# Other transfer times in a kernel's order model, and the ranks that go with them: delta rule and low-rank mixer on one core

## The chip, the core and the metric

The kernel runs on one NeuronCore of a Trainium2 chip. The metric is device microseconds (us) of one execution; a kernel's time is the median of its runs. An execution that the profiler recorded has a time of its own, and its span, from the first to the last instruction, is a little shorter than that.

## What is computed

Two blocks, one after the other, all in float32. The first is a delta-rule recurrence over 768 tokens for 4 batches with 8 heads of 48 numbers each. The second is a mixer: a low-rank product over the tokens, and then a two-layer network over the channels.

```python
k_n = k / (norm(k) + 1e-6)                     # q, k, v: (4, 8, 768, 48)
for t in range(768):
    y[:, :, t] = q_t @ state                   # state: (4, 8, 48, 48), zero at first
    state = state + beta_t * outer(k_n_t, v_t - k_n_t @ state)
x = y with the heads side by side              # (4, 768, 384)
u = x + (U @ V applied over the tokens of x)   # rank 32
out = u + relu(u @ w_ch1) @ w_ch2              # 384 -> 1536 -> 384
```

The weights of the mixer (U, V, w_ch1, w_ch2) come as 64-bit floats, and the kernel converts them to 32 bits itself.

## The kernel before

**Stages.** The recurrence is done in chunks of 64 tokens. A unit n is half of a batch: 6 chunks of all 8 heads; there are 8 units, two for each batch. For each unit the kernel loads k, q, v and a second copy of part of k that it calls z (`load`: 28 DMAs of 72 KB for a unit, 8 each for k, q and v, 4 for z), turns k and q with TensorE (`turn` in `grams`, L475, evicted at L485 to L490), forms the products within the chunks (`products`, L502, evicted at L512 to L533), inverts 32x32 triangles on VectorE (`blocks`: the transpose L584, the scaling L588, a loop of pairs L593 and L599, the transpose back L606), joins the pieces on TensorE (`joins`, L615 to L716), and multiplies the result into k and v (`prepare`, L808 and L819). Norms and beta come in through `norms` (L441 to L458; L458 scales v, and so waits for the loads of v) and `load_beta` (L410 to L425). The recurrence itself (`recur`) goes from chunk to chunk: L857 on TensorE, L870 on VectorE, L885 on TensorE, L895 on VectorE (L897 in chunk 0); `outputs` (L772, L786, L756) hangs on it. When all 12 chunks of a batch are there, `front` (L1180 to L1209) and `wide` (L1288, L1328) do the mixer in three blocks of 256 tokens for a batch; the last batch has another form for the first layer (`quick`, L1085).

**Weights.** `load_weights` brings the weights in as 14 slices: slice 0 is U, slice 1 is V (`v_sb`, 4 DMAs of 192 KB), slices 2 to 7 are w_ch1 and 8 to 13 are w_ch2 (2 DMAs of 384 KB each). `start(i)` issues slice i (L967), and can do so when slice i-1 has been issued and the buffer is free again. VectorE converts each in five steps (L989, L995, L1001, L1007, L1017), ScalarE does one between (L974). Sums of w_ch2 follow on VectorE (`sums`, L925).

**What sets the order.** Every engine executes its instructions in the order in which the program lists them, and that order is written by a planner that runs when the program is built. Each part above is a Python generator; it yields an operation with an engine and an estimated cost, or a list of events that it needs. `run()` keeps a clock for each engine, takes at each step the operation that can start first and, among those that can start within 0.18 us of the first, the one with the lowest rank. The rank is given to `begin(part, place)`, and the table `PLACES` replaces it for the parts that it names. So a table and the estimated costs make the order; what the chip does later has no say in it, and an instruction whose input is late holds all that is behind it on its engine.

A DMA's landing is estimated by `landing`: one server for all queues, 1.0 us after the issue at the earliest, a time for each packet, and 0.4 us behind it. An issue from SyncE (SP) or GpSimd (POOL) costs 0.65 us in the model. Where a load is at SP, the parts that are ready compete by rank: the loads of k, q, v, z of the first two units have the ranks 10 to 17 by default (`FIRST`), the slices of weights 22, the recurrence 1 for batch 0 and 59 for the others, `wide` 95.

Of the kernel before, what the change touches and what calls it, by code (L numbers as in the profile page):

```python
# [26 lines left out]
def kernel(  # L27
# [72 lines left out]
    def op(  # L100
        engine, cost, mode=None, take=None, give=(), lat=None, rush=None, words=0, port=None, flow=None
    ):
        return dict(
            flow=cost * 0.95 if flow is None else flow,
            e=engine, cost=cost, mode=mode, take=take, give=give, words=words + 0.4,
            port=engine == "pool" if port is None else port,
            rush=bool(give) if rush is None else rush, lat=LAT[engine] if lat is None else lat,
        )

    def need(*keys):  # L110
        return [key for key in keys if key[1] >= 0]

    def emitted(key, after=0.0):
        done[key] = state["now"] + after
        for i in awaited.pop(key, ()):
            missing[i].discard(key)
            if not missing[i]:
                woken.append(i)

    def landing(packets, each=0.0235):  # L120
        state["hw"] = max(state["hw"], state["now"] + 1.0) + packets * each / 16
        return state["hw"] + 0.4 - state["now"]

# [14 lines left out]
            waits[i] = s  # L138

    PLACES = """  # L140
    add_up b1 i1 45.09; blocks n3 111.0; blocks n4 92.42; blocks n6 79.19
    front b1 i2 64.0; front b2 i2 68.2; grams n1 i1 1.0; grams n3 i0 53.42
    grams n3 i1 -4.5; grams n4 i0 45.18; joins n0 h1 45.17; joins n1 h0 15.27
    joins n2 h0 -4.0; joins n2 h1 7.5; joins n5 h1 18.5; joins n6 h0 60.13
    joins n6 h1 68.5; joins n7 h1 62.0; last_sum b0 i2 80.69; load n0 nameq halves(0, 1) 75.0
    load n0 namez halves(0, 1) 3.5; load n1 namez halves(0, 1) 92.5; load n5 namek halves(0, 1) 49.53; load n5 namez halves(0, 1) 92.89
    load n6 namek halves(0, 1) 68.35; load_beta u0 51.5; load_beta u1 90.62; load_weights 88.45
    norms n1 113.0; norms n2 108.5; norms n3 19.33; norms n5 46.0
    outputs b0 c0 94.0; outputs b0 c3 15.7; outputs b0 c5 84.5; outputs b1 c6 56.12
    outputs b2 c0 87.54; outputs b2 c5 58.09; outputs b3 c0 -10.5; outputs b3 c1 51.03  # L150
    outputs b3 c4 81.5; outputs b3 c6 78.5; prepare n0 h0 99.5; prepare n0 h1 78.37
    prepare n1 h0 80.0; prepare n2 h0 -1.5; prepare n2 h1 6.5; prepare n3 h0 8.5
    prepare n5 h0 7.5; prepare n5 h1 44.42; prepare n6 h1 43.06; products n0 i0 j0 97.01
    products n0 i0 j1 82.0; products n0 i1 j1 110.0; products n1 i1 j1 53.69; products n2 i0 j1 73.87
    products n3 i0 j1 31.11; products n4 i0 j0 55.59; products n4 i0 j1 57.63; products n4 i1 j0 57.63
    products n5 i1 j1 3.5; products n6 i0 j1 100.7; products n6 i1 j0 73.37; products n6 i1 j1 47.56
    products n7 i1 j0 59.09; products n7 i1 j1 86.0; recur b0 31.68; recur b1 19.99
    recur b3 22.0; seed n6 -8.0; start i1 113.77; wide b0 i0 65.24
    wide b0 i2 73.0; wide b1 i2 115.5; wide b2 i1 76.0
    """  # L160
    PLACES = dict(x.strip().rsplit(" ", 1) for x in PLACES.replace("\n", ";").split(";") if x.strip())

# [115 lines left out]
    def half(i, size=L):  # L278
        return slice(L * i, L * i + size)

    def quarter(i, size=BK):
        return slice(BK * i, BK * i + size)
# [78 lines left out]
    def load(n, name, halves):  # L361
        kn, _, _, _, qn, vn, _, kz = units[n]
        t, src = dict(k=(kn, k), q=(qn, q), v=(vn, v), z=(kz, k))[name]
        b, hf = divmod(n, NU)
        yield need(("rec", n - 2), *[("x", b - 1, UC * hf + c) for c in range(UC)])
        if name == "v":
            yield need(("turned", n))
        if name == "k" and n == 0:
            e = "sp" if halves == (0,) else "act"
        else:  # L370
            e = "sp"
        for g in halves:
            if n >= NU and g:
                e = "pool"
            queue = dict(sp=nc.sync, act=nc.scalar, pool=nc.gpsimd)[e]
            for s in range(1, 4, 2) if name == "z" else range(4):
                to = dict(k=s, q=s, v=s % 2 * 2 + s // 2, z=s // 2)[name]
                yield op(e, 0.65, port=False)
                queue.dma_start(  # L379
                    out=t[half(1 - g if name == "z" else g), :, to, 0:D],  # L380
                    in_=src[b, 4 * g + s, hf * UC * L : (hf + 1) * UC * L, :].rearrange(
                        "(c t) d -> t c d", t=L
                    ),
                )
                after = landing(384)
                if name == "z" or s % 2:
                    emitted((name, n, g, s // 2), after)
        if len(halves) == 1 and halves[0]:
            yield op("act", 1.6)
            nc.scalar.sqrt(warm, warm)  # L390

    def load_beta(u):
# [3 lines left out]
        if u == 0:  # L396
            for g in range(2):
                yield op("pool", 0.6, port=False)
                nc.gpsimd.dma_start(out=beta_sb[:, g], in_=beta[:, 4 * g : 4 * g + 4])
            yield op("pool", 0.0, port=False, lat=landing(64, 0.1))  # L400
        else:
            yield need(("gram", 0))
# [150 lines left out]
    def halves(t, split):  # L553

        size = BK // split
        flat = t.rearrange("p a b -> p (a b)")[:, 0 : split * size * (BK + (split > 1))]
        return flat.rearrange("p (u x) -> p u x", u=split)[:, :, 0 : size * BK].rearrange(
            "p u (a b) -> p u a b", b=BK
        )[:, :, :, 0:size]
# [371 lines left out]
    def load_weights():  # L931
# [11 lines left out]
        def size(i):  # L943
            return NB * R if slices[i][2] == "c" else WIDE

        def start(i):
            _, src, kind = slices[i]
            n = size(i)
            before = max([x for x in range(i) if where[x] == where[i]], default=-1)
            yield need(("started", i - 1), ("freed", before), *[("joined", 0)] * (where[i] == 2))  # L950
            to = wides[where[i]][:, 0 : 2 * n]
            landed[i] = to.rearrange("p (n two) -> p n two", two=2)
            src = src.bitcast(I32)
            if kind == "c":
                pieces = [(to.rearrange("p (c r) -> p c r", c=NB), src.rearrange("(c p) r -> p c r", c=NB))]
            elif kind == "a":
                to = to.rearrange("p (t f x) -> p t f x", t=KT, f=2)
                pieces = [(to[:, :, f], src[:, :, f]) for f in range(2)]
            elif kind == "f":
                to = to.rearrange("p (a f d) -> p f a d", a=2, f=2)  # L960
                pieces = [(to[:, f], src[f]) for f in range(2)]
            else:
                pieces = [(to[quarter(j)], src) for j in range(128 // R)]
            e, queue = ("pool", nc.gpsimd) if i < 1 else ("sp", nc.sync)
            for to, of in pieces:
                yield op(e, 0.6, port=False)
                queue.dma_start(out=to, in_=of)  # L967
            emitted(("started", i))
            emitted(("wide", i), landing(256, 0.13) + 0.6)

        def raised(i, power):
            cost = 0.16 + size(i) * 0.001
# [9 lines left out]
        for i in range(len(slices)):  # L982
# [3 lines left out]
            wide = landed.pop(i)  # L986
# [349 lines left out]
    with tc.manual_schedule():  # L1336
        begin(load(0, "k", (0,)), 3)
        begin(load(0, "k", (1,)), 3)
        begin(load_beta(0), 4)
        begin(load_beta(1), 16)  # L1340
        for b in range(B):
            begin(recur(b), 1 if b == 0 else 59)
        for n in range(N):
            begin(norms(n), place_of(n))
            begin(grams(n, 0), place_of(n))
            begin(grams(n, 1), place_of(n) + 3)
            begin(blocks(n), place_of(n))
            for y, name in enumerate("kqvz"):
                if n or y:
                    begin(load(n, name, (0, 1)), FIRST.get((name, n), 20 + 4 * n + y))  # L1350
        begin(load_weights(), 40)
        begin(reserve(), 0)
        begin(weight_sums(), 97)
        begin(token_sums(), 3)
        begin(first_of_last(), 94)
        for b in range(B):
            for i in range(NG):
                begin(front(b, i), 2)
        for b in range(B):
            for i in range(NG):  # L1360
                begin(wide(b, i), 95)
        run()
# [30 lines left out]
```

## Time and profile before

| | us |
|---|---|
| median of 3 runs (lowest, highest) | 617.05 (615.25, 617.24) |
| profiled execution, its own time | 622.36 |
| its span | 620.6 |
| TensorE busy | 584.3 (94%) |
| VectorE busy | 418.3 (67%) |
| ScalarE busy | 235.6 (38%) |
| GpSimd busy | 81.5 (13%) |
| mean granted clock of TensorE | 0.929 |

A busy time is the sum of an engine's instructions in the span. The page also cuts the span into 40 slices of 15.5 us and gives the busy share of each in tenths; the granted clock of TensorE is given as a share of full speed. A wait names the instruction that waited, and the one whose end released it. The first products of the mixer (L1288) start at 125.83 us.

### The profile page before, as it was taken

How to read it: one execution, taken by the hardware profiler on the slowest of the kernel's cores; microseconds unless marked ns; L12 is line 12 of the kernel's file. 1: busy time of each engine (PE TensorE's matmuls, PEld its weight loads, DVE VectorE, ACT ScalarE, POOL GpSimd, SP SyncE). 2: the span in 40 equal slices, each digit the busy share in tenths (PEclk: the TensorE clock that was granted, in tenths of full speed). 3: DMA queues.
4: the chain of work that ended last, by engine and by line, in shares of the span. 5: the costliest groups of instructions: out<-in, count | busy, mean ns of one | idle time of the engine just before them, and what ended most of it. 6: DMA issues, size and time to landing. Idle time of an engine off the chain costs nothing.

```text
span 620.6 us, 23281 instructions
## 1 busy us (share of the span) xinstructions
PE 584.3 (94%) x10452; PEld 502.8 (81%) x10452; DVE 418.3 (67%) x1000; ACT 235.6 (38%) x462; POOL 81.5 (13%) x145
## 2 busy tenths in 40 slices
PE   5767968899999999999999999999999999999997
PEld 4666967689889889788988978988989878755997
DVE  6968979688988817899887359968972235132542
ACT  4735654651044174246327323353134131244000
POOL 3001006410000230151025032010010000000000
PEclk9766565799999999999999999999999999999999
DMA  6560549940000240370034043000000000000001
GB/s 125 107 160 5 170 154 201 207 107 2 27 5 3 61 65 4 69 131 4 3 74 91 3 96 57 11 29 3 3 28 2 27 2 2 25 2 0 6 36 36
DMA packets 72293, 33.26 MB, mean 54 GB/s; under 512 B 59649, under 2 KB 70657, under 8 KB 72193
## 3 DMA queue, kind: packets, MB, share of 16 engines
q1 hardware_dynamic: 66400, 24.98, 18.1%
q0 software_dynamic: 4192, 6.49, 4.9%
q8 instruction: 82, 1.34, 0.9%
q10 hardware_dynamic: 1600, 0.30, 0.3%
q14 instruction: 19, 0.15, 0.1%
HBM read 27.03 MB, written 4.72 MB: 51 GB/s over the span
## 4 chain that ended last, share of the span: by engine, by line
PE 84%; DVE 7%; issue 3%; ACT 2%; DMA 2%; SPq 2%; DVEq 0%; ACTq 0%
PE P L1328 27%; PE P L1288 23%; PE P L1085 7%; PE P L502 4%; PE P L475 3%; PE P L1198 3%; PE P L857 3%; DMA slot<-in_k_dram 2%; PE P L808 2%; PE P L819 2%; PE P L885 2%; PE P L772 2%; SPq L379 2%; PE P L1207 1%; PE P L786 1%
## 5 line engine op out<-in xcount | busy, mean ns | idle before, releaser
L1288 PE MATMUL P<-ut,w_sb 128*128 128x256 f32 x648 | 153.8, 386 | 0.0
L1288 PEld LDWEIGHTS P<-ut,w_sb 128*128 128x128 f32 x648 | 119.6, 191 | 19.0 <-issue 1.9
L1328 PE MATMUL P<-w_sb,hs 128*128 128x192 f32 x540 | 95.1, 330 | 0.0
L1328 PEld LDWEIGHTS P<-w_sb,hs 128*128 128x128 f32 x540 | 87.3, 190 | 1.6
L599 DVE TENSOR_TENSOR xt<-xt,prod 128x112 f32<-128x112 f32 (+21 forms) x200 | 64.5, 323 | 6.9
L1264 DVE TENSOR_TENSOR X<-X,P 128x192 f32<-128x192 f32 x84 | 29.6, 352 | 58.4 <-PE P L1328 57.3
L756 ACT COPY X<-P 64x192 f32<-64x192 f32 x96 | 30.1, 314 | 101.9 <-PE P L786 99.7
L593 DVE TENSOR_TENSOR prod<-gs,xt 128x112 f32<-128x112 f32 (+21 forms) x200 | 63.9, 320 | 4.5
L1231 ACT ACTIVATE hs<-P 128x512 f32<-128x512 f32 x54 | 32.2, 597 | 82.0 <-PE P L1288 78.6
L1328 PE MATMUL P<-w_sb,S 128*128 128x192 f32 x288 | 50.2, 329 | 0.0
L1328 PEld LDWEIGHTS P<-w_sb,S 128*128 128x128 f32 x288 | 46.7, 190 | 0.5
L475 PE MATMUL P<-ident,slot 128*128 128x128 f32 x192 | 31.5, 314 | 11.2 <-DMA slot<-in_k_dram 7.4
L870 DVE TENSOR_TENSOR z<-slot,P 128x192 f32<-128x192 f32 x44 | 15.5, 353 | 35.2 <-PE P L857 32.2
L728 ACT COPY slot<-zz 32x384 f32<-32x384 f32 x64 | 32.5, 509 | 14.9 <-DVE X L1264 8.6
L475 PEld LDWEIGHTS P<-ident,slot 128*128 128x128 f32 x192 | 25.9, 162 | 14.6 <-issue 8.1
L502 PEld LDWEIGHTS P<-slot 48*64 48x64 f32 x1536 | 28.8, 151 | 6.9 <-ACT slot L490 3.2
L502 PE MATMUL P<-slot 48*64 48x64 f32 x1536 | 32.4, 238 | 1.7 <-ACT slot L490 1.4
L1085 PE MATMUL P<-slot,w_sb 128*128 128x384 f32 x96 | 33.3, 486 | 0.0
L379 POOL DMA_DIRECT2D slot<-in_k_dram x36 | 23.6, 669 | 66.8 <-PE P L885 66.0
L1328 PE MATMUL P<-w_sb,slot 128*128 128x192 f32 x180 | 30.1, 326 | 0.0
L1328 PEld LDWEIGHTS P<-w_sb,slot 128*128 128x128 f32 x180 | 29.4, 190 | 0.5
L490 ACT COPY slot<-P 128x768 f32<-128x768 f32 x30 | 23.5, 801 | 16.5 <-PE P L475 14.4
(143 smaller groups left out, 888.1 us busy)
## 6 DMA issues: line engine op xcount, KB each, us to landing
out_dram<-X SPq DMA_DIRECT2D x22, 192.0 KB, 1.8
slot<-in_k_dram SPq DMA_DIRECT2D x56, 72.0 KB, 3.8
X<-in_moe_w_ch_dram SPq DMA_DIRECT2D x10, 384.0 KB, 5.1
wide<-in_moe_w_ch_dram SPq DMA_DIRECT2D x10, 384.0 KB, 5.3
slot<-in_q_dram SPq DMA_DIRECT2D x40, 72.0 KB, 3.7
slot<-in_v_dram SPq DMA_DIRECT2D x40, 72.0 KB, 3.2
slot<-in_k_dram POOLq DMA_DIRECT2D x36, 72.0 KB, 4.5
slot<-in_q_dram POOLq DMA_DIRECT2D x24, 72.0 KB, 5.2
```

The lines of the kernel that those rows point to most:

```text
L379: queue.dma_start(out=t[half(1 - g if name == "z" else g), :, to, 0:D], in_=src[b, 4 * g + s, hf * UC * L : (hf + 1) * UC * L, :].rearrang ...
L475: nc.tensor.transpose(p_t[:, c // 3, c % 3], t[:, c, 2 * j : 2 * j + 2].rearrange("p s d -> p (s d)"), ident,)
L502: nc.tensor.matmul(p_g[half(g ^ (par * i)), par, c], kq[rows, c, j, 0, half(g)], kq[rows, c, j, i, half(g)], start=True, stop=True,)
L593: nc.vector.tensor_tensor(out=prod, in0=gb[:, :, j : j + 1, j + 1 :].to_broadcast([128, split, m, w]), in1=xb[:, :, 0:m, j : j + 1].to_bro ...
L599: nc.vector.tensor_tensor(out=xb[:, :, 0:m, j + 1 :], in0=xb[:, :, 0:m, j + 1 :], in1=prod, op=ALU.subtract,)
L728: nc.scalar.copy(pg[quarter(i), :, at, :, a : a + BK], cut(zc, h)[quarter(i)].rearrange("p r (c j) t -> p r c j t", j=2),)
L756: nc.scalar.copy(x[half(c % 2), c // 2, 4 * D * g : 4 * D * (g + 1)].rearrange("p (j r d) -> p r j d", r=2, d=D), states(p_y)[half(g)],)
L1085: nc.tensor.matmul(to, w, t, start=start, stop=stop, skip_group_check=True)
L1231: nc.scalar.activation(hs[:, fs[0] : fs[1] + 1 : fs[1] - fs[0]], p_f, ACTF.Relu)
L1264: nc.vector.tensor_tensor(out=to, in0=to, in1=p, op=ALU.add)
L1288: nc.tensor.matmul(p_f[:, fs.index(f)], w1_sb[:, y, 256 * t + 128 * fs.index(f) :][:, 0:128], ut[:, t], start=(t == 0), stop=(t == KT - 1),)
L1328: nc.tensor.matmul(p_o, a[:, f], w2_sb[:, w, f], start=(first and f == 0), stop=(f == HF - 1), skip_group_check=True,)
```

## The change

Three things change, all of them in the planner; the operations, their sizes and their operands stay as they are.

- In `landing`, the time of one packet goes from 0.0235 to 0.0215 us (divided by 16), and each load of k, q, v or z lands 0.15 us later if it was issued by SP or ScalarE and 0.45 us later if POOL issued it.
- In `start`, each DMA of a slice of weights takes the model's DMA server for itself (256 packets of 0.095), where before the whole slice was charged once (256 packets of 0.13); the allowance behind it is 0.2 us and was 0.6.
- The table of ranks is another one. What it does not name has its default rank.

```diff
--- before.py
+++ after.py
@@ -117,7 +117,7 @@
             if not missing[i]:
                 woken.append(i)
 
-    def landing(packets, each=0.0235):
+    def landing(packets, each=0.0215):
         state["hw"] = max(state["hw"], state["now"] + 1.0) + packets * each / 16
         return state["hw"] + 0.4 - state["now"]
 
@@ -138,25 +138,28 @@
             waits[i] = s
 
     PLACES = """
-    add_up b1 i1 45.09; blocks n3 111.0; blocks n4 92.42; blocks n6 79.19
-    front b1 i2 64.0; front b2 i2 68.2; grams n1 i1 1.0; grams n3 i0 53.42
-    grams n3 i1 -4.5; grams n4 i0 45.18; joins n0 h1 45.17; joins n1 h0 15.27
-    joins n2 h0 -4.0; joins n2 h1 7.5; joins n5 h1 18.5; joins n6 h0 60.13
-    joins n6 h1 68.5; joins n7 h1 62.0; last_sum b0 i2 80.69; load n0 nameq halves(0, 1) 75.0
-    load n0 namez halves(0, 1) 3.5; load n1 namez halves(0, 1) 92.5; load n5 namek halves(0, 1) 49.53; load n5 namez halves(0, 1) 92.89
-    load n6 namek halves(0, 1) 68.35; load_beta u0 51.5; load_beta u1 90.62; load_weights 88.45
-    norms n1 113.0; norms n2 108.5; norms n3 19.33; norms n5 46.0
-    outputs b0 c0 94.0; outputs b0 c3 15.7; outputs b0 c5 84.5; outputs b1 c6 56.12
-    outputs b2 c0 87.54; outputs b2 c5 58.09; outputs b3 c0 -10.5; outputs b3 c1 51.03
-    outputs b3 c4 81.5; outputs b3 c6 78.5; prepare n0 h0 99.5; prepare n0 h1 78.37
-    prepare n1 h0 80.0; prepare n2 h0 -1.5; prepare n2 h1 6.5; prepare n3 h0 8.5
-    prepare n5 h0 7.5; prepare n5 h1 44.42; prepare n6 h1 43.06; products n0 i0 j0 97.01
-    products n0 i0 j1 82.0; products n0 i1 j1 110.0; products n1 i1 j1 53.69; products n2 i0 j1 73.87
-    products n3 i0 j1 31.11; products n4 i0 j0 55.59; products n4 i0 j1 57.63; products n4 i1 j0 57.63
-    products n5 i1 j1 3.5; products n6 i0 j1 100.7; products n6 i1 j0 73.37; products n6 i1 j1 47.56
-    products n7 i1 j0 59.09; products n7 i1 j1 86.0; recur b0 31.68; recur b1 19.99
-    recur b3 22.0; seed n6 -8.0; start i1 113.77; wide b0 i0 65.24
-    wide b0 i2 73.0; wide b1 i2 115.5; wide b2 i1 76.0
+    add_up b0 i2 95.16; blocks n1 70.71; blocks n2 50.48; blocks n3 91.9
+    blocks n5 83.33; blocks n6 58.5; blocks n7 101.5; diagonals n0 h0 20.06
+    diagonals n1 h0 92.66; diagonals n1 h1 89.08; diagonals n2 h0 93.81; diagonals n3 h1 80.5
+    gather b0 i0 h1 c0 62.71; gather b0 i0 h1 c1 62.71; gather b1 i2 h1 c1 85.96; grams n2 i0 0.0
+    grams n2 i1 53.55; grams n3 i0 75.0; grams n5 i0 28.61; grams n5 i1 51.11
+    joins n0 h0 61.46; joins n0 h1 61.46; joins n2 h0 2.5; joins n2 h1 58.05
+    joins n3 h0 75.0; joins n4 h0 45.0; joins n5 h0 -9.45; joins n6 h1 63.64
+    joins n7 h1 14.0; load n0 nameq halves(0, 1) 13.0; load n0 namev halves(0, 1) 61.71; load n1 namek halves(0, 1) 60.0
+    load n1 nameq halves(0, 1) 60.0; load n1 namez halves(0, 1) 60.0; load n2 namez halves(0, 1) 3.05; load n3 namek halves(0, 1) 72.5
+    load n4 namek halves(0, 1) 98.34; load n5 namek halves(0, 1) 14.0; load n5 nameq halves(0, 1) 26.88; load n6 nameq halves(0, 1) 4.0
+    load_beta u0 53.16; load_weights 80.74; norms n0 56.33; norms n1 58.2
+    norms n3 80.16; norms n4 17.5; norms n5 88.19; outputs b0 c1 89.69
+    outputs b0 c10 62.21; outputs b0 c7 66.28; outputs b0 c9 63.21; outputs b1 c0 24.56
+    outputs b1 c5 -3.34; outputs b1 c7 79.61; outputs b2 c0 -9.5; outputs b2 c2 91.0
+    outputs b3 c0 62.02; outputs b3 c3 80.06; outputs b3 c4 92.0; outputs b3 c6 84.74
+    prepare n0 h1 -0.5; prepare n1 h0 76.71; prepare n1 h1 76.71; prepare n2 h1 87.07
+    prepare n3 h1 3.0; prepare n4 h0 82.24; prepare n4 h1 3.5; prepare n5 h1 12.88
+    products n0 i0 j0 79.0; products n0 i1 j0 -8.5; products n0 i1 j1 -4.5; products n1 i1 j1 96.95
+    products n2 i0 j1 21.0; products n2 i1 j1 41.0; products n3 i0 j0 44.0; products n3 i0 j1 2.0
+    products n4 i1 j0 75.0; products n4 i1 j1 75.5; products n5 i0 j0 26.88; products n6 i1 j0 15.5
+    products n6 i1 j1 70.0; products n7 i1 j0 78.33; start i1 12.42; start i13 38.28
+    start i2 79.5; weight_sums 59.0; wide b2 i0 74.6
     """
     PLACES = dict(x.strip().rsplit(" ", 1) for x in PLACES.replace("\n", ";").split(";") if x.strip())
 
@@ -382,7 +385,7 @@
                         "(c t) d -> t c d", t=L
                     ),
                 )
-                after = landing(384)
+                after = landing(384) + (0.45 if e == "pool" else 0.15)
                 if name == "z" or s % 2:
                     emitted((name, n, g, s // 2), after)
         if len(halves) == 1 and halves[0]:
@@ -965,8 +968,9 @@
             for to, of in pieces:
                 yield op(e, 0.6, port=False)
                 queue.dma_start(out=to, in_=of)
+                after = landing(256, 0.095)
             emitted(("started", i))
-            emitted(("wide", i), landing(256, 0.13) + 0.6)
+            emitted(("wide", i), after + 0.2)
 
         def raised(i, power):
             cost = 0.16 + size(i) * 0.001
```

## The prediction

> **What bounds the kernel now.** I read the page's slices first, then the same by stages, the waits of the opening, and the order of time on SP and VectorE.
>
> ```profile
> PE   5767968899999999999999999999999999999997
> DVE  6968979688988817899887359968972235132542
> PEclk9766565799999999999999999999999999999999
> ```
>
> ```profile
> core 0: us, PE busy (x) PEld busy (x) DVE busy (x) ACT busy (x) POOL busy (x), PEclk, DMA share, GB/s
> 0.00:126.00 126.00, 95.61 (x2553) 83.31 (x2554) 100.13 (x227) 67.77 (x128) 26.80 (x52) 0.65 0.64 141
> 126.00:617.00 491.00, 488.30 (x7900) 419.47 (x7899) 317.83 (x772) 167.86 (x334) 54.72 (x93) 1.00 0.14 31
> 40.00:110.00 70.00, 56.73 (x1785) 52.30 (x1786) 62.88 (x130) 36.31 (x73) 15.27 (x27) 0.55 0.57 147
> ```
>
> The kernel is two stages. From 126 us on TensorE is busy 488.3 of 491 us at full clock: 2.7 us are idle, so no order gains more than that there, and a worse one can lose. Before 126 us it is idle for 126.0 - 95.6 = 30.4 us and has 0.65 of its clock; that opening is the stage an order can change. From 40 to 110 us VectorE (62.9 of 70) is fuller than TensorE (56.7). The waits of the opening:
>
> ```profile
> PE P L475 <- DMA slot<-in_k_dram: 7.4, 3, 5.1
> DVE slot L458 <- DMA slot<-in_v_dram: 4.7, 1, 4.7
> PE P L692 <- DVE zz L615: 4.6, 1, 4.6
> PE P L857 <- DVE s L897: 3.3, 1, 3.3
> ```
>
> 5.1 of the 7.4 us are the first load and stay. Lines two and three are one event: v came late, VectorE stood in front of L458, L615 behind it in its order did too, and TensorE waited for L615. In order of time:
>
> ```profile
> 12.83 11.09 SPq L379 DMA_DIRECT2D slot<-in_q_dram  x16
> 24.70 12.41 SPq L379 DMA_DIRECT2D slot<-in_v_dram  x16
> 41.61 0.93 SPq L967 DMA_DIRECT2D X<-in_moe_w_ch_dram  x2
> ```
>
> ```profile
> 33.33 0.54 DVE L667 SCALAR_TENSOR_TENSOR zz<-P,upper_rows,zz 128x96 f32<-128x96 f32 x2 [0.36 <-issue]
> 38.57 1.36 DVE L458 TENSOR_TENSOR slot<-slot,norm_rows 128x1152 f32<-128x1152 f32 x1 [4.70 <-DMA slot<-in_v_dram]
> 41.90 0.30 DVE L425 STREAM_TRANSPOSE betas<-beta_rows 128x128 f32<-128x128 f32 x1
> 44.23 0.68 DVE L588 TENSOR_TENSOR gs<-gs,cp 128x512 f32<-128x512 f32 x1
> 53.71 0.34 DVE L897 COPY s<-P 128x192 f32<-128x192 f32 x1
> ```
>
> After the stall come beta of the odd units (L425), then unit 1's triangles (L588 to 53.5 us), and behind them the first state, L897, for which TensorE waits 3.3 us.
>
> **The model's times.** They cost no instruction; they act only through the order. A load of 384 packets alone in the queue: before 1.0 + 384 x 0.0235 / 16 + 0.4 = 1.96 us after its issue, 2.61 with the 0.65 of the issue; now 2.07 and 2.72. The trace has a median of 2.7 from 13 to 24.5 us, so the old figure was 0.1 short and the new one fits. In a busy queue each load now counts 0.516 instead of 0.564. A slice of two pieces in an empty queue lands 4.04 us after its last issue, before 4.08: no longer at all. But it holds the server for 2 x 1.52 = 3.04 us instead of 2.08, and V's four pieces for 6.08. In the trace 768 KB at the 318 GB/s of 65 to 70 us are 2.4 us, at the 247 of 40 to 45 us 3.1 us: the new figure stands at the slow end, the old one below both. The Trainium skill ("DMA: Bandwidth & Descriptors", Anatomy of one DMA) has about 2.0 us plus bytes over 436 GB/s, an estimate of 2.9 us for a piece of 384 KB. That speaks against charging slices more, and by it the third edit would make the model worse and gain nothing; the medians of 5.1 and 5.3 us for such pieces here decide for the edit.
>
> **SP's order at the start.** Before, z and k of unit 1 and all of unit 1's q went ahead of unit 0's q (rank 75). Now q of unit 0 has 13, V (start i1) 12.42 instead of 113.77, z of unit 0 its default 14, and k, q, z of unit 1 have 60, v of unit 0 61.71, v of unit 1 still 17, w_ch1's first slice 79.5. By these ranks SP lists 4 k, V between the first q's, 8 q, 4 z, then 8 k, 8 q, 4 z of unit 1: 36 loads of 0.67 us (12.83 to 23.96 are 16 and a step) and 2.0 us for V, from 0.82 to 26.8 us. Then v of unit 0 ends at 32.2 us; if unit 1's q is turned in time, v of unit 1 goes ahead and it is 37.5. With 2.7 us from the start of the last issue, v lands at 34.2 or 39.6, now 38.57: between 4.4 us better and 1.0 worse. k of unit 1 was issued by 12.8 us; now 16 loads and V stand before its 8, so that it ends at 18.8 and lands near 21, some 6 us later; its triangles wait anyway for unit 0's (to 26.8 us), so this costs nothing while that cover holds, and up to 6 us without it.
>
> **VectorE and TensorE to 65 us.** load_beta u1 goes from 90.62 to 16 and norms n1 from 113 to 58.2. Unit 1's Gram columns are laid out at 32.3 us; L444 to L449 took 1.2 us, L588 0.7: its substitution (8.6 us, 44.9 to 53.5) can begin near 34.5, up to 10 us earlier, inside the stall. Against this, blocks n1 falls from 14 to 70.7, behind the recurrence (31.68 to 1), so L897 would no longer stand behind it. What TensorE can take of this are its idle times: 4.1 us in 35 to 40, 3.5 in 50 to 55, 7.6 in all. From 55 to 75 it is full and slow, and earlier inputs bring nothing:
>
> ```profile
> 55.00:60.00 5.00, 4.96 (x224) 4.58 (x224) 4.07 (x8) 4.03 (x9) 0.82 (x2) 0.50 0.03 7
> 65.00:70.00 5.00, 5.00 (x121) 5.00 (x120) 4.90 (x9) 2.42 (x5) 0.00 (x0) 0.50 0.98 318
> ```
>
> The gain lies between -7.6 and +1.0; I take -4, near the half, because where v lands has both answers. V's conversion (five steps, 4.0 us, 56.85 to 64.9) can move into VectorE's hole at 34 us; TensorE being full there, I take -1 (0 to -4).
>
> These two rows also weigh a rule. The Trainium skill ("TensorE: Matmul & The Clock Gate", Part 1) says that one window of about 3.4 us of sustained work brings the full clock. Here TensorE is busy 5.00 of 5 us and still has 0.50. By that rule, closing the holes would also double the clock, and half of the 56.7 us of the stage 40 to 110, some 25 us (an estimate), could go. By the rows nothing of it is to be had with these small products, and the sum has none of it.
>
> **The rest of the ranks.** recur b0 at 1 and prepare at 1 and -0.5 (99.5, 78.37) draw chunks 3 to 5 forward: chunk 2's L870 is at 58.09 us, chunk 3's at 81.85. But chunk 6 needs unit 1, whose share of TensorE then comes later. Nothing shows which ends last: 0, ends -4 and +4. Loads of later units queue with slices at 90 to 126 us; k of unit 2 cost TensorE 1.9 us at 118.8: 0, ends -1.9 and +2. From 126 us on: 0, ends -1 and +4, by the 2.7 us that are lost now.
>
> **Sum.** -4 - 1 = -5 us, so the profiled execution's 622.36 would be 617.4. That execution is 5.3 us above the median; taken from the median 617.05 the forecast is 612.0.
>
> **Rivals.** *Slower: VectorE's conversions end last.* w_ch1's first slice now stands behind all the opening loads (37.5 us, before 41.6: no later), but conversions have rank 80.74 behind a recurrence at rank 1. They take 4.0 us a slice, and 12 of 14 are done by 126 us in 100 of 126 busy us. The last sums of w_ch2 (L925) end at 145.4 us, and the products that read them stand some 6 us later. If more than one slice slips beyond that, each costs TensorE 4.0 us: one or two past it make 617 + 4 = 621 to 617 + 8 = 625. For it: VectorE is the fuller engine; against: it has 26 us idle in the opening. Chance 0.37 with all that loses in the later ranks. *No change:* TensorE full at half clock from 55 to 75 us swallows what is gained before: 617. This also covers that the change does not do what it says, as slices land no later in an empty queue (4.04 against 4.08). Chance 0.10. *Larger gain:* both holes close (-7.6), the chunks come forward (-4) and unit 2's k is in time (-1.9): -13.5, 603.5. It is the end of the faster case, which has 0.53 in all.
>
> **Numbers.** The measurement tells 0.3% (1.9 us) from no change: faster is below 615.2, slower above 618.9. Range 604 to 625: from the larger gain to two slices late; within the faster case alone 604 to 615. A little over half of the weight lies below, since one stall is seen that the new order can close; no more, since of the other ranks I can only bound the effect.
>
> **What would show it.** Right: V's DMAs on SP before 10 us; no VectorE wait of more than 2 us at L458; L425 for the odd units before 33 us; L897 before 50 us; first L1288 near 121 us; under 4 us idle behind it. Wrong: L458 still waiting 4 us; idle TensorE before L1328 with VectorE at L1007 or L925; or many small waits of TensorE after 130 us.

## The result and the profile after

The changed kernel takes 621.96 us (median of 4 runs, 620.68 to 622.79), the kernel before 616.25 us beside it (615.25 to 617.24): a ratio of 1.008, with a 95% interval of 1.0059 to 1.0101. It is 0.8% slower, 5 to 6 us, where 5 us less were forecast; the time lies inside the range of 604 to 625. The profiled execution took 622.25 us with a span of 620.6, the same span as the first profile of before. So the two profiles that lie side by side do not hold the difference.

The lines below carry numbers of the changed kernel, where a line stands 3 or 4 further down: L461 is what L458 was, L900 is L897, L1292 is L1288. First the page's slices, then the stages.

```profile
PE   4775977799999999999999999999999999999997
DVE  6959898999989888489827897888223414132542
PEclk9666556999999999999999999999999999999999
```

```profile
0.00:126.00 126.00, 92.78 (x2597) 82.84 (x2598) 103.95 (x241) 65.21 (x126) 26.33 (x51) 0.67 0.64 141
126.00:617.00 491.00, 487.21 (x7857) 418.46 (x7855) 313.10 (x759) 169.35 (x336) 54.93 (x94) 1.00 0.15 31
```

From 126 us on TensorE is idle for 491.0 - 487.2 = 3.8 us, 1.1 more than before: the late stage is nearly as full as it was. The opening is not shorter. Its waits, and the order of time on SP and VectorE:

```profile
PE P L478 <- DMA slot<-in_k_dram: 7.9, 5, 5.2
DVE slot L461 <- issue: 5.0, 1, 5.0
PE P L692 <- DVE zz L670: 3.5, 1, 3.5
DVE power L993 <- DMA X<-in_moe_w_ch_dram: 2.6, 1, 2.6
```

```profile
5.90 2.00 SPq L970 DMA_DIRECT2D wide<-in_moe_V_dram  x4
7.94 3.80 SPq L382 DMA_DIRECT2D slot<-in_q_dram  x5
11.88 9.99 SPq L382 DMA_DIRECT2D slot<-in_k_dram  x12
30.01 11.73 SPq L382 DMA_DIRECT2D slot<-in_v_dram  x16
41.85 2.10 SPq L970 DMA_DIRECT2D X<-in_moe_w_ch_dram  x2
```

```profile
30.59 0.29 DVE L428 STREAM_TRANSPOSE betas<-beta_rows 128x128 f32<-128x128 f32 x1
35.58 0.54 DVE L993 TENSOR_SCALAR power<-wide 128x768 int32<-128x768 int32 x1
45.27 1.36 DVE L461 TENSOR_TENSOR slot<-slot,norm_rows 128x1152 f32<-128x1152 f32 x1 [5.00 <-issue]
46.78 1.36 DVE L461 TENSOR_TENSOR slot<-slot,norm_rows 128x1152 f32<-128x1152 f32 x1
50.17 0.65 DVE L591 TENSOR_TENSOR gs<-gs,cp 128x512 f32<-128x512 f32 x1
65.79 0.36 DVE L900 COPY s<-P 128x192 f32<-128x192 f32 x1 [1.48 <-ACT zz L657]
```

```profile
126.33 1.46 PE L1292 MATMUL P<-ut,w_sb 128*128 128x256 f32 x6
```

The stall in front of the scaling of v is still there, 5.0 us long, and stands 6.7 us later. Beta of the odd units and V's conversion did move ahead of it (30.59 and 35.58 us). Unit 1's scaling L591 begins at 50.17 us where before it began at 44.23, and the first state of the recurrence comes at 65.79 us where before it came at 53.71. The order of the program's DMAs explains the length: SP issues six of unit 0's eight v, then all eight of unit 1's, then unit 0's last two, so that unit 0's scaling waits for the last of all sixteen. The profile names no releaser for this wait (`issue`); that it is v's landing is read from the order of the DMAs here, and tested below by moving v.

### The profile page after: what moved, and what is told of

It reads as the page before. It is cut to its first block, busy times and chain, and to the rows that moved or that the text cites. A ratio compares the mean times of both kernels' runs of the same rounds, so it can differ in the third digit from the quotient of the medians.

```text
span 620.6 us, 23297 instructions
## 1 busy us (share of the span) xinstructions
PE 580.3 (94%) x10452; PEld 501.3 (81%) x10452; DVE 417.4 (67%) x1000; ACT 234.6 (38%) x462; POOL 81.3 (13%) x145
## 4 chain that ended last, share of the span: by engine, by line
PE 76%; DVE 14%; DMA 4%; SPq 3%; issue 2%; ACT 1%; DVEq 0%; ACTq 0%
PE P L1332 27%; PE P L1292 22%; PE P L1089 7%; SPq L382 3%; PE P L505 3%; PE P L860 2%; PE P L1202 2%; PE P L478 2%; DVE prod L596 2%; DVE xt L602 2%; DMA X<-in_moe_w_ch_dram 2%; PE P L888 2%; PE P L775 1%; PE P L789 1%; PE P L811 1%
## 5 line engine op out<-in xcount | busy, mean ns | idle before, releaser
L1292 PE MATMUL P<-ut,w_sb 128*128 128x256 f32 x648 | 153.7, 386 | 0.0
L1292 PEld LDWEIGHTS P<-ut,w_sb 128*128 128x128 f32 x648 | 118.9, 190 | 18.2 <-issue 1.2
L1255 DVE TENSOR_TENSOR S<-hs 128x384 f32<-128x384 f32 x18 | 9.9, 553 | 29.8 <-ACT hs L1235 29.8
```

The source lines that it names most:

```text
L1292: nc.tensor.matmul(p_f[:, fs.index(f)], w1_sb[:, y, 256 * t + 128 * fs.index(f) :][:, 0:128], ut[:, t], start=(t == 0), stop=(t == KT - 1),)
```

## The experiments

**Other executions of the kernel before.** Nothing is edited.

> The kernel before, unchanged, for a second profile. Theory A, the clock of the opening: the first profiled execution of before had an unlucky opening (0.51 of the clock at 120 to 125 us, 5.3 us above the median), and a usual one has the full clock from about 110 us on and its first L1288 at 119 to 122 us; span 614 to 616. Theory B, the profile adds to this kernel: first L1288 again at 125 to 126.5 us and a span near 620.

> The same kernel a third time, since the clock of the opening may differ from execution to execution. Theory A: first L1288 at 119 to 122 us in most profiles, and where it is later, the granted clock in 110 to 126 us is lower by as much. Theory B: 125 to 126.5 us each time.

> The kernel before once more, for a profile of an execution near its median. The spread of its runs (615 to 621) comes from the opening: first L1288 at 121 us for a run of 616.5, and for any run its time less the start of L1288 is 495 to 497 us.

They took 620.43, 619.57 and 617.19 us. With the other profiles of this study:

| execution | wait before L667 | wait before the first scaling of v | scaling begins | first products L1288 | granted clock 110 to 126 us | span | span less first products |
|---|---|---|---|---|---|---|---|
| before, first profile | 0.36 | 4.70 | 38.57 | 125.83 | 0.71 | 620.6 | 494.8 |
| before_1 | 0.90 | 3.96 | 39.13 | 124.12 | 0.91 | 618.7 | 494.6 |
| before_2 | 2.89 | 1.25 | 38.25 | 124.23 | 0.89 | 617.9 | 493.7 |
| before_3 | 3.07 | 1.46 | 37.94 | 120.38 | 1.00 | 615.5 | 495.1 |
| changed | other order | 5.00 | 45.27 | 126.33 | 1.00 | 620.6 | 494.3 |

L667 is the instruction that stands just ahead of the scaling in VectorE's order of the kernel before. The profile of before_3, whose time is near the median, in the page's slices and in the order of time on VectorE and TensorE, and one line of the first profile:

```profile
PEclk8655555999999999999999999999999999999999
35.93 0.54 DVE L667 SCALAR_TENSOR_TENSOR zz<-P,upper_rows,zz 128x96 f32<-128x96 f32 x2 [3.07 <-issue]
37.94 1.36 DVE L458 TENSOR_TENSOR slot<-slot,norm_rows 128x1152 f32<-128x1152 f32 x1 [1.46 <-DMA slot<-in_v_dram]
119.04 1.44 DVE L515 SCALAR_TENSOR_TENSOR slot<-P,even,slot 128x192 f32<-128x192 f32 x4
120.38 1.46 PE L1288 MATMUL P<-ut,w_sb 128*128 128x256 f32 x6
```

```profile
122.59 0.74 DVE L515 SCALAR_TENSOR_TENSOR slot<-P,even,slot 128x192 f32<-128x192 f32 x2 [2.46 <-ACT slot L512]
```

Theory A holds in its main point: the span less the start of the first products is 493.7 to 495.1 us in all five, so the time is decided when the mixer starts. It missed in two: only one of three profiles began by 122 us, and in before_1 the clock of 110 to 126 us does not account for all of the delay. The wait in front of the scaling must not be read alone. It is 4.7 us in the first profile and 1.3 to 1.5 us in the two fastest, but there VectorE has stood 2.9 and 3.1 us just before it, in front of L667. Together it stands 4.1 to 5.1 us in all four, and the scaling begins within 1.2 us. So the stall is no accident of the first profile, and it is not where that execution lost its time: before_3 begins the scaling only 0.6 us earlier, but its first products 5.5 us earlier. At 118 us the two are still 1.2 us apart; the rest comes where the first profile waits 2.46 us for the products of unit 3's k (L515), and has 0.51 of the clock from 120 to 125 us where before_3 has 1.00.

**Each half of the change alone.** `times_only` has the new times and the old table, `ranks_only` the old times and the new table.

```diff
 # times_only, against the changed kernel
-    add_up b0 i2 95.16; blocks n1 70.71; blocks n2 50.48; blocks n3 91.9
...
+    add_up b1 i1 45.09; blocks n3 111.0; blocks n4 92.42; blocks n6 79.19
...
 # ranks_only, against the kernel before
-    add_up b1 i1 45.09; blocks n3 111.0; blocks n4 92.42; blocks n6 79.19
...
+    add_up b0 i2 95.16; blocks n1 70.71; blocks n2 50.48; blocks n3 91.9
...
```

> The new transfer times with the old table of ranks. Theory A (the ranks cost the time): 614 to 619. Theory B (a table fits only the times it was found with, so that either half alone is worse than both kernels): 624 or more. Theory C (the times misplace work): 620 to 624, as the whole change.

> The old transfer times with the new table of ranks. Theory A (the ranks cost the time): 620 to 624. Theory B (a table fits only the times it was found with): 624 or more. Theory C (the times misplace work): 614 to 619.

Measured: 651.92 us (1.0579, interval 1.0513 to 1.0646) and 637.96 us (1.0327, 1.0273 to 1.0381), beside 616.6. Theory B, clearly: a table of ranks fits only the costs it was found with. The times alone start the products at 127.3 us and lose most behind that; the ranks alone start them at 139.2. Neither half can be called the one that costs the time, and whole re-planning is too coarse a tool to find it.

**The order held, v taken from another queue.** The next kernels don't plan: a list of the planner's picks and PSUM banks, taken from the changed kernel (or from the one before), stands in for the choice, so that every engine keeps its order apart from what is named. Their lines stand 143 to 145 further down (L606 or L604 is L461).

```diff
-            at, i = min(picks)
+            at, i = next((t, x) for them in some.values() for t, x in them if x[1] == ORDER[k])
...
             if n >= NU and g:
                 e = "pool"
+            if n < NU and name == "v":
+                e = "pool"      # before_v_pool: "pool" if n or g else "sp"
```

In `ORDER`, unit 0's eight v stand ahead of unit 1's.

> The changed kernel with every engine's order kept as it is, but v of units 0 and 1 issued by POOL, unit 0's first, where SP issued it from 30 to 41.7 us. Theory A (v's late landing holds VectorE 5.0 us in front of L461, and the opening passes that on): the wait at L461 falls below 1 us, L1292 starts 3 to 5 us earlier than 126.3, time 617 to 619. Theory B (the opening ends with other work, the weights or TensorE at half clock, so that the stall is free): L1292 within 1.5 us of where it was, time 620.5 or more.

> The kernel before with its order kept, but half of unit 0's v and all of unit 1's v issued by POOL, and unit 0's before unit 1's, so that L458 need not wait 4.7 us. Theory A (the stall is on the path): wait under 1.5 us, 2 to 4 us faster than before, 613 to 615. Theory B (the stall is free, since TensorE is full at half clock from 55 to 75 us): within 1.5 us of before.

`after_v_pool`: 618.37 us beside 616.92, 1.0019 (1.0004 to 1.0034). VectorE and TensorE in order of time (L663 is L518, L754 is L609):

```profile
29.95 0.74 DVE L663 SCALAR_TENSOR_TENSOR slot<-P,even,slot 128x192 f32<-128x192 f32 x2 [2.53 <-ACT slot L660]
31.59 2.08 DVE L754 STREAM_TRANSPOSE zz<-xt 128x1024 f32<-128x1024 f32 x1
41.89 1.35 DVE L606 TENSOR_TENSOR slot<-slot,norm_rows 128x1152 f32<-128x1152 f32 x1
121.61 1.46 PE L1437 MATMUL P<-ut,w_sb 128*128 128x256 f32 x6
```

No wait is left in front of L606, the products start 4.7 us earlier, and three quarters of the loss are gone: 1.0080 - 1.0019 = 0.0061 of 0.0080, 3.8 us. Theory A. The move also frees SP, so that the first slice of w_ch1 is issued at 30.29 us and not at 41.85; but VectorE converts it only at 63.88 us (68.20 in the changed kernel), so this is not what brings the gain. There is a new wait of 2.53 us in the first row, for the products of unit 1's k. In the changed kernel the same step has no wait, and it stands 3 us earlier:

```profile
26.97 0.74 DVE L518 SCALAR_TENSOR_TENSOR slot<-P,even,slot 128x192 f32<-128x192 f32 x2
```

So the new wait belongs to the experiment, where POOL issues unit 0's v while SP is still issuing unit 1's k (to 22 us; k then lands after 3.9 us, the median from 11.5 to 22 us, against 3.3 in the changed kernel):

```profile
18.07 5.22 POOL L527 DMA_DIRECT2D slot<-in_v_dram  x8 [12.17 <-DMA slot<-in_k_dram]
```

`before_v_pool`: 616.12 us, 0.9987 (0.9965 to 1.0009), with 0.68 us of wait left. That is no difference that can be told, and theory A's 2 to 4 us are not there. Where they went, VectorE and TensorE show:

```profile
35.34 1.36 DVE L603 TENSOR_TENSOR slot<-slot,norm_rows 128x1152 f32<-128x1152 f32 x1 [0.68 <-DMA slot<-in_v_dram]
115.53 0.96 DVE L1162 SCALAR_TENSOR_TENSOR w_sb<-X,power 128x768 f32<-128x768 f32 x1
119.22 1.59 DVE L660 SCALAR_TENSOR_TENSOR slot<-P,even,slot 128x192 f32<-128x192 f32 x4 [2.74 <-ACT slot L657]
120.70 1.46 PE L1433 MATMUL P<-ut,w_sb 128*128 128x256 f32 x6
```

The scaling begins 2.6 us earlier than in before_3, and VectorE keeps the lead for 80 us: the last step of the conversion ahead of the wait is at 115.53 us, in before_3 at 117.96. Then it waits 2.74 us for the products of unit 3's k (TensorE has waited 2.06 us for that k to land), where before_3 waits for nothing, and the first products come at 120.70 us as against 120.38. So in the kernel before the time won at the scaling is lost again at the next late load. This is read from one profile of each kernel, both of executions near their medians.

**Only the order of v on SP.** v stays on SP, unit 0's eight go first.

```diff
 # ORDER, SP's part
-  v0 x6, v1 x8, v0 x2
+  v0 x8, v1 x8
```

> The changed kernel with its order kept, but on SP all of unit 0's v go before unit 1's (now two of unit 0's eight come after them). Theory A (what counts is how long VectorE stands): the two scalings L461 stand one behind the other in VectorE's order, and the second still needs the last v that SP issues, so the stall moves to the second one, and the time stays at 621 to 623. Theory B (what counts is when unit 0 gets its v): 618 to 619, as with POOL.

620.87 us, 1.0067 (1.0037 to 1.0098): not to be told from the change itself, though a little under the 621 to 623 named. VectorE:

```profile
40.48 1.35 DVE L604 TENSOR_TENSOR slot<-slot,norm_rows 128x1152 f32<-128x1152 f32 x1
45.36 1.36 DVE L604 TENSOR_TENSOR slot<-slot,norm_rows 128x1152 f32<-128x1152 f32 x1 [3.42 <-issue]
```

The scaling of unit 0's v comes 4.8 us earlier and it helps little; the wait, 3.42 us of it, goes to the second scaling, which the new order puts directly behind the first. So what costs is that VectorE stands, whichever unit it stands for.

**V's four DMAs put back.** Both kernels move them on SP behind the last z of unit 1; the first has v on POOL as well.

```diff
 # ORDER, SP's part
-  k0 x4, q0 x3, V x4, q0 x5, z0 x4, k1 x8, q1 x8, z1 x4
+  k0 x4, q0 x8, z0 x4, k1 x8, q1 x8, z1 x4, V x4
```

> As after_v_pool (618.4), and the four DMAs of V go on SP behind the last of unit 1's z, where the change put them between the first q's. Theory A (V's early DMAs hold up q and k of the first units, the rest of the loss): L606's first transpose back about 1.5 us earlier than 28.6, time 616.5 to 617.5. Theory B (the rest of the loss is the order of the work itself): 618 to 619.

> The changed kernel with its order kept, v on SP as in the change, and only V's four DMAs moved on SP behind the last of unit 1's z. v is issued no earlier by this, since V still stands ahead of it. Theory A (the two losses add): V costs its 2.5 us here too, 619 to 620. Theory B (the stall for v covers it): VectorE reaches L461 earlier and waits longer there, up to 7 us, and the time stays at 621 to 622.5.

With v on POOL: 615.92 us beside 616.53, 0.999 (0.9977 to 1.0003). The rest of the loss is gone:

```profile
29.14 2.10 DVE L754 STREAM_TRANSPOSE zz<-xt 128x1024 f32<-128x1024 f32 x1
39.84 1.35 DVE L606 TENSOR_TENSOR slot<-slot,norm_rows 128x1152 f32<-128x1152 f32 x1
119.44 1.46 PE L1437 MATMUL P<-ut,w_sb 128*128 128x256 f32 x6
```

The time is theory A's, better than named, but the transpose back is not at 27.1 us. It is at 29.14, which is 2.45 us before its place in after_v_pool: k of unit 1 comes earlier and the wait of 2.53 us is what goes. Without the move of v, `after_V_late` takes 621.27 us beside 617.76, 1.0054 (1.0033 to 1.0076), and VectorE reads:

```profile
45.35 1.36 DVE L604 TENSOR_TENSOR slot<-slot,norm_rows 128x1152 f32<-128x1152 f32 x1 [5.57 <-issue]
```

The wait grows from 5.00 to 5.57 us and the scaling stands where it stood: theory B by the profile, though the wait did not grow to 7. The time does not settle it: 621.27 us lies in B's range, but beside a kernel before that ran 1.5 us slower than beside the change, and the two ratios, 1.0054 and 1.0080, have intervals that overlap. What V costs when v comes from POOL (2.5 us at the transpose) it does not cost in the change itself, where the products of unit 1's k start at 26.97 us with V ahead and at 27.55 without it.

So the stall in front of the scaling is the loss: in `after_v_pool_V_late` the scaling begins 5.4 us earlier than in the changed kernel, the first products 6.9 us earlier, and the time is that of the kernel before. The two steps, 0.0061 for v and then 0.0029 for V, are 0.0090 against the 0.0080 lost. The fastest kernels here are `after_v_pool_V_late` and `before_v_pool`; neither can be told from the kernel before.

## Why the prediction was wrong, step by step

**What bounds it: right.** In the five profiles of the table the first products are followed by 493.7 to 495.1 us, and in the five with an order held by 493.9 to 494.8. Gains and losses of these kernels are all in the opening; only the halves alone lost time in the late stage too (649.4 - 127.3 = 522.1 us in times_only, 637.2 - 139.2 = 498.0 in ranks_only).

**SP's order: the step that failed, a term with the wrong sign.** The sum took -4 from closing the stall, with v to land at 34.2 or 39.6 us; L461 began at 45.27, after a wait of 5.0 us, which is the prediction's first sign of being wrong. Three things were missed. SP came to v at 30.01 us, not 26.8: V's own issues took the 2.0 us charged, but the 12 loads behind it took 9.99, 0.83 each instead of 0.67, and the rows shown in the prediction already have 0.69 and 0.78 (11.09 and 12.41 us for 16). Second, I had two cases, unit 0's v first or unit 1's first. The program has a third: six, then the other eight, then two, because the rank of 17 took over as soon as unit 1's q was turned. (The z that went ahead of unit 0's q before was unit 0's, not unit 1's as the prediction has it; the sum does not rest on that.) The last of unit 0's v was issued at 41.1 us. Third, it landed 3.9 us after its issue and not 2.7, with the first slice of w_ch1 right behind it. Removing the stall from the change gave 3.8 us (after_v_pool), so the term measured +3.8 where I took -4 from bounds of -7.6 and +1.0.

**The size of the gain: wrong too, and about a third of the error.** The error is some 10 us, from -5 forecast to +5. Even with the stall closed -4 is not there: after_v_pool_V_late, the new order without it, is at 0.999. And in the kernel before, before_v_pool takes the wait for v down to 0.68 us and has a ratio of 0.9987: 0.8 us, somewhere between 2.2 faster and 0.6 slower. The prediction asked what TensorE could take of the gain between 35 and 65 us, and not what VectorE would wait for next; that was the load of unit 3's k at 115 us. (The 1.9 us at 118.8 us that the prediction gives to unit 2's k are this load of unit 3.) The prediction also noted that the first profile lay 5.3 us above the median without asking where; set beside before_3, they lay behind 118 us for the most part, and not in the stall.

**V's early place: the cover held, the gain is not there.** The prediction had k of unit 1 coming 6 us later and covered by unit 0's triangles. It came later (SP ends it at 21.9 us, not 18.8), and VectorE did not wait for it in the change; only with v's loads on POOL at the same time did it cost 2.5 us. V's conversion did go into the gap (35.58 us), as forecast, and its -1 is not to be seen in the time.

**VectorE's order: half right.** Beta of the odd units came before 33 us (30.59). The substitution did not begin near 34.5: the new order puts both scalings of v ahead of it, so that it waits for v too. L900 was forecast before 50 us and is at 65.79, since it now stands behind the whole substitution, which ends at 60.4.

**The model's times: right on sizes, wrong on what they do.** I argued from landings of 5 us that charging the slices more fits the trace. But next to nothing waited for them. SP and VectorE in before_3, and its waits:

```profile
74.82 0.90 SPq L967 DMA_DIRECT2D wide<-in_moe_w_ch_dram  x2
86.80 0.56 DVE L989 TENSOR_SCALAR power<-wide 128x768 int32<-128x768 int32 x1
DVE power L989 <- DMA X<-in_moe_w_ch_dram: 1.2, 1, 1.2
DVE power L989 <- DMA wide<-in_moe_w_ch_dram: 0.4, 1, 0.4
```

The slice issued at 74.82 us is used at 86.80, 12 us later (another one, of 63.33, at 69.16), and all the slices together cost VectorE 1.6 us. The prediction's 2.9 us for a piece rests on a sum that the Trainium skill ("DMA: Bandwidth & Descriptors", Anatomy of one DMA) states for DMAs issued by GpSimd. SP's pieces here landed after medians of 5.1 and 5.3 us. The planner sees it otherwise. Holding each order and letting the planner add up its own clock, which is an estimate and no time of the chip, the old order goes from 610.1 to 615.9 us when the slices get their new time, and stays at 610.1 when only the loads do. The new table is worth 615.2 by the new times, 0.7 better than the old order, and 621.4 by the old ones, 11.3 worse; the chip says 5 to 6 worse. So the new times made the planner see some 6 us of waits in the old order that the chip doesn't have, and a table that avoids them looked like a gain. That it was this which led the search is argued from the planner's figures; no run on the chip shows it.

**The rivals.** The slower one had the time (621 to 625, chance 0.37) and the wrong mechanism. The last sums of w_ch2 end at 161.4 us, 16 later than before, and TensorE has no wait for them. The Trainium skill's rule on the clock ("TensorE: Matmul & The Clock Gate", Part 1), that one window of sustained work brings the full clock, is again not borne out by small products: TensorE is busy 5.00 of 5 us from 65 to 75 us of the changed kernel, at a clock of 0.50, and with the stall taken out (after_v_pool) the clock of 40 to 80 us is 0.59, against 0.54.

## What to carry to other kernels

Before a stall in a profile is costed, ask what the engine would wait for next if it were gone: before_v_pool won 2.6 us at the scaling and lost them 80 us later at the next late load. Compare where an instruction starts, and not only the wait written beside it: 4.70 and 1.46 us of wait stood in front of scalings that began 0.6 us apart, because the engine had stood one instruction earlier instead. And ask how far a profiled execution lies from the median, and in which stretch. A cost in an order model matters where something waits for what it costs; making it truer for transfers that have 6 to 12 us to spare can move the order for nothing, and a table of ranks belongs to the costs it was found with (3% and 6% lost with the other's). On one queue, look at which consumer stands behind the last of a group of transfers, and put a group that is waited for whole ahead of the next.

## What the runs showed of the hardware

Loads of 72 KB that SP issues right behind V's four transfers of 192 KB land late. First the loads that the changed kernel issues from 7.9 to 12 us, then those that after_V_late issues in the same stretch, where V is not ahead, with the last column in us to landing:

```profile
slot<-in_q_dram SPq DMA_DIRECT2D x5, 72.0 KB, 5.8
```

```profile
slot<-in_k_dram SPq DMA_DIRECT2D x5, 72.0 KB, 3.3
slot<-in_q_dram SPq DMA_DIRECT2D x3, 72.0 KB, 4.1
```

From 22 to 27.3 us of the changed kernel such loads take 2.5 us. And the same program has a granted clock of 0.71 to 1.00 at 110 to 126 us from one execution to another, with its first products between 120.4 and 125.8 us; the kernel before ran from 613.9 to 620.75 us in the runs beside these experiments, so that one execution says little about 1%.
